# Chunked attention and a gated feed-forward layer in one kernel: blocks cut along the batches, v of block 1 loaded in two parts around a quarter of w_out, and AV of block 1 in other PSUM banks

## The chip, the cores and the metric

The kernel runs on one core of a Trainium2 chip. The metric is device time in microseconds (us) of one execution. Executions that follow each other differ by one to three us here (the kernel before took 308.97 to 311.54 us in one group of runs), so kernels are compared by several executions on the same chip. All executions told of here were classed as fast; none is compared with a slow one. The profile is one such execution; its span runs from the core's first to its last instruction and is about 2 us shorter than the time (308.6 of 310.3 us for the kernel before).

Names: TensorE (PE) multiplies matrices, and its weight loads (PEld) are listed apart; VectorE is DVE, ScalarE is ACT, GpSimd is POOL, SyncE is SP, which issues most of the loads here. In PSUM the kernel uses eight banks; it calls four of them A and four F.

## The reference

Softmax attention inside chunks of 64 tokens, then a feed-forward layer with a Swish gate:

```python
batch, n_heads, seq, head_dim = (8, 8, 576, 64)      # 9 chunks of 64 in a batch
scores = 1 / sqrt(64) * (q_c @ k_c.T)                # for each chunk by itself
attn = softmax(scores); x = (attn @ v_c)             # x: 4608 tokens x 512
h = x @ w_in                                         # w_in: 512 x 2048
g = h * sigmoid(beta * h)
out = g @ w_out                                      # w_out: 2048 x 512, out: 4608 x 512
```

All inputs and the output are float32 in HBM. The kernel casts to bfloat16 on the chip.

## The kernel before

The 72 chunks are worked in nine blocks of 8 chunks (512 tokens). A block needs: loads of q, k, v; casts on POOL; transposes of q and k (on TensorE for blocks 0 to 2; later by DMA, after which POOL or DVE copies the result into order); scores; exp; AV (attn @ v); normalisation on DVE; a transpose ("turn") of x; then 16 groups of four matmuls on w_in (`mm1`) and 16 groups of four on w_out (`mm2`). From block 2 on, the attention of a block is woven into the matmul groups of earlier blocks. Blocks 0 and 1 come while weights and inputs still arrive.

Every operation is recorded with a time in a schedule (`at(time, ...)`); sorted by it, the operations form one queue for each engine, and each engine runs its queue in order. Tiles that one engine writes and another reads become semaphore waits.

Before the change, blocks follow the running number of the chunk. A batch has 9 chunks, so most blocks straddle two batches, and a pair of chunks that does so is loaded as two DMAs of 64 partitions each ("half-height") instead of one of 128:

```python
def chunk_runs(blk):
    g, end, runs = 8 * blk, 8 * blk + 8, []
    while g < end:
        b, c = divmod(g, CPB)                 # CPB = 9 chunks in a batch
        n = min(end - g, CPB - c)
        runs.append((b, c, n, g - 8 * blk))
        g += n
    return runs

def chunk_pairs(blk):
    out = []
    for b, c, n, at in chunk_runs(blk):
        end = at + n
        while at < end:
            m = 2 if at % 2 == 0 and at + 2 <= end else 1
            out.append((b, c, m, at))
            at, c = at + m, c + m
    return out
```

AV of a block comes in two parts (u = 0, 1: heads 0 to 3 and 4 to 7), each of 32 small matmuls that write all four banks of A. Normalisation reads these banks and writes x:

```python
def attend(blk, u, ps=A, psname="A"):
    sa = blk % NVA
    for cc in range(4):
        ... # hb, w, g: 8 matmuls of 64x64 by 64x65
                P.op("pe", f, reads=[K("E", 2 * u + hb, v=blk), K("v_bf", sa, cc, v=blk),
                                     K("ones", sa)],
                     writes=[K(psname, 2 * g + cc // 2, v=("o", blk, u))])

def normalize(blk, u, ps=A, psname="A"):
    ... # DVE: reciprocal of the row sums, then one tensor_tensor into x_sb
```

The schedule of block 1 and of the weights that matters here:

```python
for j in range(4):
    at(-97, load_w_in, j)
    at((-43, 1.5, 5.5, 9.5)[j], cast_w_in, j, ("pool",) * 4)
    at((-42, 1.7, 5.7, 9.7)[j], load_w_out, j)
    at((16.1, 20, 24, 25)[j], cast_w_out, j, ("pool",) * 4)
at(-43.5, load_qk, 1, 0)
at(-43.5, load_qk, 1, 1)
at(-43.5, load_v, 1)
...
for blk, t in ((1, 10), (2, 28)):
    for i in range(4):
        at(25 if blk == 2 else t + 0.1 * i, cast_qk, blk, i // 2, i % 2, "pool")
        at(t + 0.9 * i if blk == 2 else 10.5 + 0.8 * i, transpose_pe, blk, i // 2, i % 2, A, "A", ("act", "dve")[i % 2])
        at(26 if blk == 2 else t + 4, cast_v, blk, "pool", i)
for hp in range(4):
    at(14.9 + 0.6 * (hp // 2), scores, 1, hp)
for bank in range(4):
    at((15.1, 15.2, 15.7, 15.8)[bank], exp, 1, bank)
at(17.1, attend, 1, 0)
at(17.2, normalize, 1, 0)
at(18.1, attend, 1, 1)
at(18.2, turn_pe, 1, 0, F, "F", 0, "act")
at(18.3, normalize, 1, 1)
at(19.1, turn_pe, 1, 1, F, "F", 1, "act")
```

The recorder notes every operation that reads a tile, so that whoever overwrites the tile later waits for all its readers. Each such reader counts up its engine's semaphore:

```python
for key, v in writes:
    add(self.writer.get(key), op["queue"] == "pool")
    for r in self.readers.get(key, ()):
        add(r, False)
for key, v in reads:
    self.readers.setdefault(key, []).append(op)
```

The softmax here doesn't subtract the row's maximum and nothing guards it: scores larger than these inputs give would overflow.

## Time and profile before

| | before |
|---|---|
| time, median of three (lowest to highest) | 310.36 us (310.19 to 310.51) |
| profiled span | 308.6 us |
| TensorE busy from 31.8 to 51.8 us | 12.58 of 20 us |
| TensorE busy from 100 to 120 us | 19.74 of 20 us |

From the page of the kernel before: the clock granted to TensorE in tenths over 40 slices of 7.7 us, and the chain of work that ended last, as shares of the span by engine and by line.

```profile
PEclk9999985999999999999999999999999999999999
...
PE 80%; SPq 9%; DMA 6%; issue 1%; POOL 1%; DVE 1%; ACT 0%
PE F L456 40%; PE F L441 36%; SPq L257 6%; DMA wstage<-in_moe_w_out_dram 4%; DMA vstage<-in_v_dram 2%; SPq L265 2%; PE A L389 2%; PE A L367 2%; SPq L274 1%; POOL w_out_bf L306 1%; PE A L341 1%; DVE x_sb L405 0%; PE A L423 0%; DVE g L449 0%; ACT tt L446 0%
```

The chain is TensorE's (L456 and L441 are the two feed-forward matmuls), except for a stretch of loads at the start. And the clock drops in one place, between 39 and 54 us (by the trace's records to half, from 43.7 to 53.9 us). The table of stretches shows the same place from another side; its columns are named in its first line.

```profile
core 0: us, PE busy (x) PEld busy (x) DVE busy (x) ACT busy (x) POOL busy (x), PEclk, DMA share, GB/s
31.80:51.80 20.00, 12.58 (x201) 7.31 (x201) 10.02 (x13) 10.00 (x15) 11.94 (x19) 0.80 1.00 291
100.00:120.00 20.00, 19.74 (x181) 9.18 (x183) 10.38 (x16) 9.39 (x15) 13.11 (x11) 1.00 0.70 183
```

Late in the kernel nothing is to be won: TensorE is full. Early, over 7 us are idle. TensorE's timeline of that place follows; the columns are start, duration, engine, line, operation, tiles, shape, count, and in brackets the idle time before it and what ended it. L367 are scores, L389 AV, L423 turns.

```profile
40.32 0.44 PE L367 MATMUL A<-qkO 64*64 64x64 bf16 x32
41.75 0.19 PE L389 MATMUL A<-v_bf,E 64*64 64x65 bf16 x1 [0.98 <-ACT E L374]
42.63 0.32 PE L389 MATMUL A<-v_bf,E 64*64 64x65 bf16 x16 [0.69 <-ACT E L374]
43.12 0.32 PE L389 MATMUL A<-v_bf,E 64*64 64x65 bf16 x15 [0.17 <-ACT E L374]
45.48 0.66 PE L389 MATMUL A<-v_bf,E 64*64 64x65 bf16 x32 [2.04 <-DVE x_sb L405]
46.07 1.03 PE L423 MATMUL F<-identity,x_sb 128*128 128x128 bf16 x8
48.41 1.03 PE L423 MATMUL F<-identity,x_sb 128*128 128x128 bf16 x8 [1.31 <-DVE x_sb L405]
49.23 1.06 PE L441 MATMUL F<-xT,w_in_bf 128*128 128x512 bf16 x2
50.55 1.04 PE L441 MATMUL F<-xT,w_in_bf 128*128 128x512 bf16 x2 [0.26 <-ACT xT L312]
```

AV part 0 writes the A banks while exp still reads scores from them, so it follows the exps bank by bank. AV part 1 waits 2.04 us until normalisation of part 0 has emptied A. The turns wait for their own normalisations. Nothing else is in TensorE's queue there.

This stretch also begins late, for the last keys of block 1 come late. POOL's timeline:

```profile
35.60 1.04 POOL L314 CAST qkcast<-qkstage 128x1024 bf16<-128x1024 f32 x1 [1.35 <-DMA qkstage<-in_k_dram]
```

### The profile page before, as it was taken

To read this page: it belongs to the slowest core of one execution; us is meant where nothing else is said; L and a number is where in the kernel's file an instruction comes from. 1 tells how busy PE (TensorE), PEld (TensorE's weight loads), DVE (VectorE), ACT (ScalarE), POOL (GpSimd) and SP (SyncE) were. 2 spreads that over 40 slices of the span, in tenths; PEclk is the share of its full clock that TensorE was granted. 3 is DMA by queue.
4 is the path that set the end of the run, shared out by engine and by line. 5 is a ranking of instruction groups with operands and counts; after the bars stand their busy time and mean duration, and the time that the engine had idled before them with its cause. 6 is when DMAs were issued, how large, how long until landed. Compare 5 with 4: busy or idle time off the path is not lost.

```text
span 308.6 us, 5739 instructions
## 1 busy us (share of the span) xinstructions
PE 281.7 (91%) x2415; PEld 134.9 (44%) x2448; DVE 137.2 (44%) x194; ACT 150.6 (49%) x230; POOL 117.0 (38%) x130
## 2 busy tenths in 40 slices
PE   1679747999899999999999999999999999999995
PEld 1444423454444444444444444444444444444442
DVE  1347742353573643364346436533553364434300
ACT  2537643456356444745464446455544645455411
POOL 1348548742490674077229220951570000000000
PEclk9999985999999999999999999999999999999999
DMA  7999999989999389929964997499531022000121
GB/s 198 273 385 328 180 346 368 250 257 234 240 291 219 88 211 270 203 68 286 244 155 102 294 202 189 78 340 230 127 79 36 34 70 69 36 34 34 38 100 68
DMA packets 106153, 55.96 MB, mean 181 GB/s; under 512 B 78992, under 2 KB 97424, under 8 KB 106128
## 3 DMA queue, kind: packets, MB, share of 16 engines
q1 hardware_dynamic: 98880, 46.15, 61.7%
q10 hardware_dynamic: 7248, 9.45, 8.9%
q8 instruction: 19, 0.31, 0.4%
q14 instruction: 6, 0.05, 0.1%
HBM read 36.71 MB, written 9.44 MB: 150 GB/s over the span
## 4 chain that ended last, share of the span: by engine, by line
PE 80%; SPq 9%; DMA 6%; issue 1%; POOL 1%; DVE 1%; ACT 0%
PE F L456 40%; PE F L441 36%; SPq L257 6%; DMA wstage<-in_moe_w_out_dram 4%; DMA vstage<-in_v_dram 2%; SPq L265 2%; PE A L389 2%; PE A L367 2%; SPq L274 1%; POOL w_out_bf L306 1%; PE A L341 1%; DVE x_sb L405 0%; PE A L423 0%; DVE g L449 0%; ACT tt L446 0%
## 5 line engine op out<-in xcount | busy, mean ns | idle before, releaser
L449 DVE SCALAR_TENSOR_TENSOR g<-tt,F 128x512 bf16<-128x512 bf16 x144 | 98.9, 687 | 128.9 <-ACT tt L446 128.7
L446 ACT ACTIVATE tt<-F,beta_half 128x512 bf16<-128x512 f32 x144 | 98.9, 687 | 116.9 <-PE F L441 113.0
L441 PE MATMUL F<-xT,w_in_bf 128*128 128x512 bf16 x576 | 148.3, 383 | 0.9 <-DVE g L449 0.6
L456 PE MATMUL F<-w_out_bf,g 128*128 128x512 bf16 x543 | 140.3, 381 | 2.6 <-issue 1.1
L456 PEld LDWEIGHTS F<-w_out_bf,g 128*128 128x128 bf16 x576 | 56.1, 99 | 67.4 <-issue 1.4
L441 PEld LDWEIGHTS F<-xT,w_in_bf 128*128 128x128 bf16 x576 | 54.3, 98 | 64.4 <-issue 1.7
L314 POOL COPY qkO<-qkT 128x1024 bf16<-128x1024 bf16 x22 | 42.7, 1981 | 59.6 <-DMA qkT<-qkcast 28.9
L314 POOL CAST qkcast<-qkstage 128x1024 bf16<-128x1024 f32 x32 | 34.7, 1092 | 27.0 <-DMA qkstage<-in_q_dram 13.2
L461 ACT ACTIVATE ostage<-F 128x512 f32<-128x512 f32 x36 | 21.5, 597 | 18.6 <-PE F L456 18.4
L314 POOL CAST v_bf<-vstage 128x512 bf16<-128x512 f32 x36 | 21.1, 611 | 14.9 <-DMA vstage<-in_v_dram 14.9
L374 ACT ACTIVATE E<-A 128x512 bf16<-128x512 f32 x36 | 20.6, 591 | 1.8 <-PE A L367 1.4
L405 DVE TENSOR_TENSOR x_sb<-A,rec 128x1024 bf16<-128x1024 f32 x17 | 20.8, 1224 | 0.6
L389 PE MATMUL A<-v_bf,E 64*64 64x65 bf16 x544 | 8.6, 200 | 4.1 <-ACT E L374 2.1
L341 PE MATMUL F<-identity,qkcast 128*128 128x128 bf16 x32 | 4.1, 311 | 8.3 <-DVE qkcast L314 6.4
L294 POOL CAST w_in_bf<-wstage 128x512 bf16<-128x512 f32 x16 | 9.1, 613 | 5.4 <-DMA wstage<-in_moe_w_in_dram 5.4
L306 POOL CAST w_out_bf<-wstage 128x512 bf16<-128x512 f32 x16 | 9.1, 613 | 5.1 <-DMA wstage<-in_moe_w_out_dram 5.1
L389 PEld LDWEIGHTS A<-v_bf,E 64*64 64x64 bf16 x544 | 6.3, 111 | 10.7 <-issue 6.6
L367 PEld LDWEIGHTS A<-qkO 64*64 64x64 bf16 x576 | 6.8, 112 | 8.2 <-issue 5.7
L367 PE MATMUL A<-qkO 64*64 64x64 bf16 x576 | 8.7, 200 | 1.2 <-ACT qkO L312 1.2
L402 DVE RECIPROCAL rec<-A 128x16 f32<-128x16 f32 x17 | 4.3, 254 | 7.4 <-PE F L441 4.0
L312 ACT ACTIVATE xT<-F 128x1024 bf16<-128x1024 bf16 x3 | 3.1, 1023 | 8.2 <-PE F L423 8.2
L341 PEld LDWEIGHTS F<-identity,qkcast 128*128 128x128 bf16 x32 | 3.1, 141 | 9.0 <-DVE qkcast L314 6.8
(31 smaller groups left out, 46.7 us busy)
## 6 DMA issues: line engine op xcount, KB each, us to landing
out_dram<-ostage ACTq DMA_DIRECT2D x36, 256.0 KB, 2.1
qkstage<-in_q_dram SPq DMA_DIRECT2D x32, 256.0 KB, 4.4
qkstage<-in_k_dram SPq DMA_DIRECT2D x32, 256.0 KB, 5.2
vstage<-in_v_dram SPq DMA_DIRECT2D x32, 256.0 KB, 6.5
wstage<-in_moe_w_in_dram SPq DMA_DIRECT2D x4, 1024.0 KB, 10.6
wstage<-in_moe_w_out_dram SPq DMA_DIRECT2D x4, 1024.0 KB, 10.6
qkstage<-in_q_dram SPq DMA_DIRECT2D x8, 128.0 KB, 4.6
qkstage<-in_k_dram SPq DMA_DIRECT2D x8, 128.0 KB, 5.1
```

Of the source, the lines that this page charges most:

```text
L257: return e.dma_start(qkstage[r:r + 64 * m, s, which, :, at // 2, :], a)
L306: P.op(eng, lambda e, d=dst, a=src: e.tensor_copy(d, a), reads=[K("wstage", s, v=4 + j)], writes=[K("w_out", 4 * j + i)])
L314: P.op(eng, lambda e: e.tensor_copy(dst, src), reads, writes)
L367: return e.matmul(A[64 * g:64 * g + 64, 2 * u + hb, col:col + 64], kT[r, 2 * cc + g, :], qT[r, 2 * cc + g, :])
L374: P.op("act", lambda e: e.activation(E[:, bank, :], A[:, bank, :], AF.Exp, scale=0.125), reads=[K("A", bank, v=("s", blk))], writes=[K("E" ...
L389: return e.matmul(ps[64 * half:64 * half + 64, bank, col:col + 65], E[r, 2 * u + hb, 256 * w + 64 * cc:256 * w + 64 * cc + 64], v_bf[r, sa ...
L405: P.op("dve", lambda e: e.tensor_tensor(x_sb[:, u, :, :, :].rearrange("p g c (h d) -> p (g c h) d", h=2).rearrange("p (b t) d -> p b t d", ...
L441: P.op("pe", lambda e, c=c: e.matmul(F[:, bank, :], w_in_bf[:, c, 128 * t:128 * t + 128], x_of(sx, c), start=(c == 0), stop=(c == NC - 1)) ...
L446: P.op("act", lambda e: e.activation(tt[:, T % 3, :], F[:, bank, :], AF.Tanh, scale=beta_half[:, t:t + 1]), reads=[K("F", bank, v=("h", T) ...
L449: P.op("dve", lambda e: e.scalar_tensor_tensor(g2[:, sg, t, :], tt[:, T % 3, :], 1.0, F[:, bank, :], ALU.add, ALU.mult), reads=[K("F", ban ...
L456: P.op("pe", lambda e, t=t: e.matmul(F[:, bank, :], g2[:, sg, t, 128 * s:128 * s + 128], w_out_bf[:, t, :], start=(t == 0), stop=(t == NT ...
L461: P.op("act", lambda e: e.activation(ostage[:, N % NOS, :], F[:, bank, :], AF.Copy, scale=0.5), reads=[K("F", bank, v=("o", N))], writes=[ ...
```

## The change

The intent, as read from the diff: (1) make blocks equal to batches (their first 8 chunks), with one block, number 5, for the eight last chunks, so that blocks 0 to 4 and 6 to 8 are loaded without half-height DMAs; (2) load v of block 1 in two parts, with the first quarter of w_out between them; (3) write AV part 0 of block 1 to the F banks, which are idle there (in the trace before nothing uses them from 41.84 us, the end of a gate product, to the turn at 46.07), so that it need not wait for all exps nor hold up part 1; (4) fill waits of that attention with two early groups on w_out. The output rows follow the new blocks.

```diff
+        REST = 5
         def chunk_pairs(blk):
-            ... (walks over chunk_runs)
+            if blk == REST:
+                return [(b, CPB - 1, 1, b) for b in range(B)]
+            return [(blk - (blk > REST), c, 2, c) for c in range(0, 8, 2)]
-        def load_v(blk):
+        def load_v(blk, us=(0, 1)):          # the heads of parts us alone; cast_v likewise
         ... (keys of vstage and v_bf now name the part u; output rows by batch)
-            at((-42, 1.7, 5.7, 9.7)[j], load_w_out, j)
-            at((16.1, 20, 24, 25)[j], cast_w_out, j, ("pool",) * 4)
+            at((-42.8, 1.7, 5.7, 9.7)[j], load_w_out, j)
+            at((15, 20, 24, 25)[j], cast_w_out, j, ("pool",) * 4)
-        at(-43.5, load_v, 1)
+        at(-42.9, load_v, 1, (0,))
+        at(-42.7, load_v, 1, (1,))
-                at(t + 0.9 * i if blk == 2 else 10.5 + 0.8 * i, transpose_pe, ...)
-                at(26 if blk == 2 else t + 4, cast_v, blk, "pool", i)
+                at(t + 0.6 + 0.9 * i if blk == 2 else 10.5 + 0.8 * i, transpose_pe, ...)
+                if blk == 2:
+                    at(26, cast_v, 2, "pool", i)
+                else:
+                    at(t + 4, cast_v, 1, "pool", i, (0,))
+                    at(t + 6.5, cast_v, 1, "pool", i, (1,))
-            at(14.9 + 0.6 * (hp // 2), scores, 1, hp)
+            at(15.4, scores, 1, hp)
-            at((15.1, 15.2, 15.7, 15.8)[bank], exp, 1, bank)
-        at(17.1, attend, 1, 0)
-        at(17.2, normalize, 1, 0)
+            at(15.5 + 0.1 * bank, exp, 1, bank)
+        at(17.1, attend, 1, 0, F, "F")
+        at(17.2, normalize, 1, 0, F, "F")
-            at(24.5 + (0, 0, 3.5, 3.6)[n] if n < 4 else 24.5 + n, mm2, 0, s, part, 2 + s % 2)
+            at((18.5, 19.5, 24.5, 24.6)[n] if n < 4 else 24.5 + n, mm2, 0, s, part, 2 + s % 2)
```

More of the change, by code (lines that the diff above doesn't have):

```diff
@@ L200, in bass_chunk_attention__then__act_swish_beta_kernel @@
         F = es.enter_context(nc.psum_tensor("F", [128, 4, 512], F32))
-        def chunk_runs(blk):
-            g, end, runs = 8 * blk, 8 * blk + 8, []
-            while g < end:
-                b, c = divmod(g, CPB)
-                n = min(end - g, CPB - c)
-                runs.append((b, c, n, g - 8 * blk))
-                g += n
-            return runs
-        def chunk_pairs(blk):
-            out = []
-            for b, c, n, at in chunk_runs(blk):
-                end = at + n
-                while at < end:
-                    m = 2 if at % 2 == 0 and at + 2 <= end else 1
-                    out.append((b, c, m, at))
-                    at, c = at + m, c + m
-            return out
+        REST = 5
+        def chunk_pairs(blk):
+            if blk == REST:
+                return [(b, CPB - 1, 1, b) for b in range(B)]
+            return [(blk - (blk > REST), c, 2, c) for c in range(0, 8, 2)]
         def make_constants():
@@ L258, in load_qk @@
                 P.dma(queue, f, writes=[K("qkstage", s, which, at + i, v=blk) for i in range(m)])
-        def load_v(blk):
-            s = blk % NVS
+        def load_v(blk, us=(0, 1)):
+            s, h = blk % NVS, slice(4 * us[0], 4 * us[-1] + 4)
             for b, c, m, at in chunk_pairs(blk):
@@ L264, in f @@
                     r = 64 * (at % 2)
-                    return e.dma_start(vstage[r:r + 64 * m, s, at // 2, :, :],
-                                       v[b][:, 64 * c:64 * (c + m), :].rearrange("h t d -> t h d"))
-                P.dma("sp", f, writes=[K("vstage", s, at + i, v=blk) for i in range(m)])
+                    return e.dma_start(vstage[r:r + 64 * m, s, at // 2, h, :],
+                                       v[b][h, 64 * c:64 * (c + m), :].rearrange("h t d -> t h d"))
+                P.dma("sp", f, writes=[K("vstage", s, u, at + i, v=blk)
+                                       for u in us for i in range(m)])
         def load_w_in(j):
@@ L350, in transpose_pe, with cast_v @@
                       [K("qkO", hp, which, half, v=blk) for hp in range(4)])
-        def cast_v(blk, eng, cc):
-            s, sa = blk % NVS, blk % NVA
-            copy_cast(eng, v_bf[:, sa, cc, :, 0:64], vstage[:, s, cc, :, :],
-                      [K("vstage", s, 2 * cc + g, v=blk) for g in range(2)],
-                      [K("v_bf", sa, cc, v=blk)])
+        def cast_v(blk, eng, cc, us=(0, 1)):
+            s, sa, h = blk % NVS, blk % NVA, slice(4 * us[0], 4 * us[-1] + 4)
+            copy_cast(eng, v_bf[:, sa, cc, h, 0:64], vstage[:, s, cc, h, :],
+                      [K("vstage", s, u, 2 * cc + g, v=blk) for u in us for g in range(2)],
+                      [K("v_bf", sa, u, cc, v=blk) for u in us])
         def scores(blk, hp):
@@ L392, in f @@
                                     v_bf[r, sa, cc, 4 * u + 2 * w + hb, 0:65])
-                            P.op("pe", f, reads=[K("E", 2 * u + hb, v=blk), K("v_bf", sa, cc, v=blk),
+                            P.op("pe", f, reads=[K("E", 2 * u + hb, v=blk), K("v_bf", sa, u, cc, v=blk),
                                                  K("ones", sa)],
@@ L463, in mm2 @@
                      reads=[K("F", bank, v=("o", N))], writes=[K("o", N % NOS, v=N)])
-                n0 = 512 * blk + 128 * s
-                P.dma("act", lambda e: e.dma_start(out[n0:n0 + 128, :], ostage[:, N % NOS, :]),
+                rows = out.rearrange("(b t) d -> b t d", b=B)
+                if blk == REST:
+                    rows = rows[2 * s:2 * s + 2, 512:S, :]
+                else:
+                    rows = rows[blk - (blk > REST), 128 * s:128 * s + 128, :]
+                P.dma("act", lambda e: e.dma_start(rows, ostage[:, N % NOS, :]),
                       reads=[K("o", N % NOS, v=N)])
@@ L516, in bass_chunk_attention__then__act_swish_beta_kernel @@
                 at(25 if blk == 2 else t + 0.1 * i, cast_qk, blk, i // 2, i % 2, "pool")
-                at(t + 0.9 * i if blk == 2 else 10.5 + 0.8 * i, transpose_pe, blk, i // 2, i % 2, A, "A", ("act", "dve")[i % 2])
-                at(26 if blk == 2 else t + 4, cast_v, blk, "pool", i)
+                at(t + 0.6 + 0.9 * i if blk == 2 else 10.5 + 0.8 * i, transpose_pe, blk, i // 2, i % 2, A, "A", ("act", "dve")[i % 2])
+                if blk == 2:
+                    at(26, cast_v, 2, "pool", i)
+                else:
+                    at(t + 4, cast_v, 1, "pool", i, (0,))
+                    at(t + 6.5, cast_v, 1, "pool", i, (1,))
         for hp in range(4):
-            at(14.9 + 0.6 * (hp // 2), scores, 1, hp)
+            at(15.4, scores, 1, hp)
         for bank in range(4):
-            at((15.1, 15.2, 15.7, 15.8)[bank], exp, 1, bank)
-        at(17.1, attend, 1, 0)
-        at(17.2, normalize, 1, 0)
+            at(15.5 + 0.1 * bank, exp, 1, bank)
+        at(17.1, attend, 1, 0, F, "F")
+        at(17.2, normalize, 1, 0, F, "F")
         at(18.1, attend, 1, 1)
```

## The prediction

> **What bounds the kernel now.** TensorE. The chain of waits gives it 80% of the 308.6 us span. By the table of stretches it is over 97% busy from 100 us on (0.86 us per four-matmul group). The loss is early: TensorE is busy 12.58 of the 20 us from 31.8 to 51.8. By the timeline it waits 1.75 us at 34.9 (last key cast on GpSimd, released by its load), then from 40.7 to 49.2 it only takes pieces of block 1's attention. AV part 0 writes the four A banks, so it waits for all four exps (43.1); AV part 1 waits 2.0 us for part 0's normalisation to empty A; the turns wait for normalisations. The records grant half a TensorE clock from 43.7 to 53.9 us. [...] the seven w_out matmuls at 51.8 take 2.73 us.
>
> Loads are the second limit. By the landings, block 1 needs q and k until 35.5 and v until 39.6 us, with six of its 15 loads half-height (64 partitions), and v in 256-byte packets at about 217 GB/s against 350 for q and k and 385 for weights. Half-height v loads run at 150, then a hole at 35 us. w_out lands at 44.1, 46.8, 49.4, 52.2.
>
> **What the change does.** Arithmetic and bytes stay. Block 1 needs 8 full-height q/k loads instead of 10, and v in two halves around the first w_out quarter. Estimates from these rates and durations:
> - last key landed at 33, cast by 34.4 instead of 36.6: about 1.5 us;
> - v half 0 landed by 36, first w_out quarter 38–39.5, v half 1 40–41.5, the last quarter about 49 instead of 52;
> - AV part 0 into F starts when exps 0 and 1 are done; AV part 1 into A no longer waits for normalisation, but for exps 2 and 3 and for the cast of v half 1 behind four w_out casts (2.3 us): about 42.4 us instead of 46.1;
> - two w_out groups (0.86 us each) fill the waits for normalisation and turns; two more follow.
>
> TensorE then reaches the first transposes of block 2 at about 54 instead of 57.8 us with four more groups (3.5 us) done. That is 7 us, all critical, if the clock stays whole; a quiet window still halving it (chance 0.3) loses about 2.5 us again.
>
> Later: the half-height loads gather in block 5 (24 of 128 KB). That block's data had about 8 us in hand before its scores; the extra issues (0.6 us each) cost about 4. Block 3's transposed q and k landed at 81.1 and will be about 4 us earlier, while TensorE comes 7 us earlier.
>
> **Predicted: 303.8 us, range 301.3 to 306.8.** Faster by over 2% 0.55, within 2% 0.43, slower 0.02.
>
> **What would show it.** Right: TensorE busy 31.8–51.8 rises to 15–17 us; the 2.0 us wait of AV on x_sb is gone; no half clock, or a shorter one; last w_out quarter by 50 us. Wrong: AV part 1 long waiting for v_bf; half clock still about 10 us; new waits at block 3's order copies (near 80 us) or at block 5's scores (near 142 us).
>
> **What would make it wrong.** The first w_out quarter delaying v half 1; the clock; DVE blocked on block 3's transpose, which holds up its g work in order.

The passage cut from it, where the cut is marked, gave a rule for the clock. No term of its sum is cut: the 7 us, and the 2.5 us at a chance of 0.3, stand. What the trace of the kernel before shows of the clock: from 40.27 to 43.68 us TensorE is busy 1.32 of 3.41 us, and its clock is half for the 10.24 us after that; the seven w_out matmuls of 2.73 us begin in it, and the eight w_in matmuls that follow them, at the full clock again from 54.38 us on, took 1.89. The chance of 0.3 and the cost of about 2.5 us are estimates, and the prediction does not say from which numbers. The rates of the loads are those of the landings in the same trace: in block 0, v loads of 256 KB land 1.2 us apart (217 GB/s) and most q and k loads 0.75 us apart (350), and the later quarters of w_out, 1 MB each, land 2.7 us apart (385). While the half-height v loads of block 1 run, from 32.5 to 34.5 us, the table of stretches gives 136 to 170 GB/s, and 31 from 35.0 to 35.5 us.

## The result, and the profile after

Ratios below are the mean time of one kernel's fast runs over that of the other's fast runs of the same rounds, so they are not quite the ratio of the medians that stand beside them.

| | before | after |
|---|---|---|
| time, median (lowest to highest) | 310.38 us (310.19 to 310.51, 4 runs) | 305.75 us (305.31 to 307.16, 4 runs) |
| ratio to before, 95% interval | | 0.9859 (0.9827 to 0.9892) |
| profiled span | 308.6 us | 303.5 us |
| TensorE busy from 31.8 to 51.8 us | 12.58 us | 17.86 us |
| half clock near 43 us | 10.2 us | 3.4 us |

The changed kernel is 4.6 us faster, inside the predicted range and 2 us short of its middle. The gain is 1.4%, so it lies in the class "within 2%", to which the prediction gave 0.43, and not in "over 2%", to which it gave 0.55. The same lines of the page after:

```profile
PEclk9999989999999999999999999999999999999999
...
PE 88%; DVE 3%; ACT 3%; DMA 2%; issue 1%; SPq 1%; ACTq 0%
PE F L432 41%; PE F L447 40%; PE A L358 3%; PE A L380 2%; DVE x_sb L396 2%; DMA qkstage<-in_k_dram 2%; SPq L247 1%; PE A L332 1%; PE F L414 1%; ACT E L365 1%; ACT tt L437 1%; DVE g L440 1%; PE F L380 1%; DVE qkO L305 0%; ACTq L460 0%
```

The chain no longer runs over loads of v and w_out; of its loads only k is left with a share. The stretches after:

```profile
31.80:51.80 20.00, 17.86 (x223) 10.46 (x221) 10.39 (x15) 11.44 (x17) 13.85 (x26) 0.91 1.03 318
100.00:120.00 20.00, 19.84 (x181) 9.30 (x184) 8.85 (x13) 9.07 (x15) 14.10 (x12) 1.00 0.69 185
```

TensorE's timeline after (L358 scores, L380 AV, L414 turns, L447 w_out, L432 w_in):

```profile
37.83 1.51 PE L358 MATMUL A<-qkO 64*64 64x64 bf16 x64
39.80 0.22 PE L380 MATMUL F<-v_bf,E 64*64 64x65 bf16 x4 [0.46 <-POOL w_out_bf L297]
40.24 0.52 PE L380 MATMUL F<-v_bf,E 64*64 64x65 bf16 x28 [0.22 <-ACT E L365]
41.45 1.29 PE L380 MATMUL A<-v_bf,E 64*64 64x65 bf16 x32 [0.69 <-POOL v_bf L305]
42.99 0.91 PE L414 MATMUL F<-identity,x_sb 128*128 128x128 bf16 x8 [0.25 <-DVE x_sb L396]
44.12 1.48 PE L447 MATMUL F<-w_out_bf,g 128*128 128x512 bf16 x3 [0.22 <-issue]
45.40 1.06 PE L414 MATMUL F<-identity,x_sb 128*128 128x128 bf16 x8
46.26 1.19 PE L447 MATMUL F<-w_out_bf,g 128*128 128x512 bf16 x4
47.28 1.03 PE L432 MATMUL F<-xT,w_in_bf 128*128 128x512 bf16 x4
```

The wait of 2.04 us before AV part 1 is gone; part 1 now waits 0.69 us for the cast of the second half of v, and is then held to the pace of its four casts. (The "POOL w_out_bf" before AV part 0 is an attribution to read with care: this AV does not read w_out at all, and the casts of its half of v had ended by 36.3 us, so that wait is for an exp.) The loads came as estimated: by the trace's landing times the last key at 33.2 us (35.5 before), the first half of v at 35.9, the first quarter of w_out at 38.7, the second half of v at 40.8, and the last quarter of w_out at 49.8 (52.2 before).

From there on, TensorE keeps what it won but for one new wait before the scores of block 2:

```profile
60.66 0.61 PE L332 MATMUL A<-identity,qkcast 128*128 128x128 bf16 x8
61.10 1.03 PE L447 MATMUL F<-w_out_bf,g 128*128 128x512 bf16 x4
61.97 1.03 PE L432 MATMUL F<-xT,w_in_bf 128*128 128x512 bf16 x4
63.81 0.45 PE L358 MATMUL A<-qkO 64*64 64x64 bf16 x32 [0.81 <-DVE qkO L305]
```

DVE's timeline after shows why. The last transposes (L332) are done at 61.3 us, but DVE, which runs its queue in order, first has to do a gate product (L440) that itself waits for ACT, and only then copies the keys (L305):

```profile
61.93 0.69 DVE L440 SCALAR_TENSOR_TENSOR g<-tt,F 128x512 bf16<-128x512 bf16 x1 [1.84 <-ACT tt L437]
62.54 1.22 DVE L305 COPY qkO<-A 128x1024 bf16<-128x1024 bf16 x1
```

The order is the diff's doing: it moved the transposes of block 2 by 0.6 in the schedule, which put the last one, and the copy after it, behind one more group on w_in.

The comparison is simplest with three marks from the traces, which split the early part of the kernel: the start of block 1's scores, the start of block 3's scores, and the end. From block 3's scores to the end every kernel here needs 218 to 219 us, apart from the last experiment (219.4).

| trace | scores of block 1 start | from there to scores of block 3 | half clock in that stretch |
|---|---|---|---|
| before | 38.98 | 51.04 | 10.2 |
| after | 37.83 | 46.85 | 3.4 |

So 1.15 us come from arriving earlier at block 1's scores and 4.19 us from the stretch after it.

### The profile page after: what moved, and what is told of

The parts are those of the page before. It is cut to its first block, busy times and chain, and to the rows that moved or that the text cites. A ratio compares the mean times of both kernels' runs of the same rounds, so it can differ in the third digit from the quotient of the medians.

```text
span 303.5 us, 5750 instructions
## 1 busy us (share of the span) xinstructions
PE 280.7 (92%) x2415; PEld 135.4 (45%) x2448; DVE 136.8 (45%) x194; ACT 151.0 (50%) x230; POOL 117.6 (39%) x134
## 4 chain that ended last, share of the span: by engine, by line
PE 88%; DVE 3%; ACT 3%; DMA 2%; issue 1%; SPq 1%; ACTq 0%
PE F L432 41%; PE F L447 40%; PE A L358 3%; PE A L380 2%; DVE x_sb L396 2%; DMA qkstage<-in_k_dram 2%; SPq L247 1%; PE A L332 1%; PE F L414 1%; ACT E L365 1%; ACT tt L437 1%; DVE g L440 1%; PE F L380 1%; DVE qkO L305 0%; ACTq L460 0%
## 5 line engine op out<-in xcount | busy, mean ns | idle before, releaser
L440 DVE SCALAR_TENSOR_TENSOR g<-tt,F 128x512 bf16<-128x512 bf16 x144 | 98.7, 686 | 127.6 <-ACT tt L437 127.4
L432 PE MATMUL F<-xT,w_in_bf 128*128 128x512 bf16 x576 | 146.5, 380 | 0.7 <-DVE g L440 0.6
L447 PE MATMUL F<-w_out_bf,g 128*128 128x512 bf16 x543 | 140.4, 381 | 2.7 <-issue 1.3
L447 PEld LDWEIGHTS F<-w_out_bf,g 128*128 128x128 bf16 x576 | 55.8, 98 | 65.4 <-issue 0.8
L432 PEld LDWEIGHTS F<-xT,w_in_bf 128*128 128x128 bf16 x576 | 54.2, 98 | 64.7 <-DVE g L440 2.0
L305 POOL COPY qkO<-qkT 128x1024 bf16<-128x1024 bf16 x22 | 42.7, 1984 | 59.6 <-DMA qkT<-qkcast 20.3
L305 POOL CAST qkcast<-qkstage 128x1024 bf16<-128x1024 f32 x32 | 33.0, 1046 | 24.8 <-DMA qkstage<-in_k_dram 9.9
L305 POOL CAST v_bf<-vstage 128x512 bf16<-128x512 f32 (+1 forms) x40 | 23.4, 616 | 14.0 <-DMA vstage<-in_v_dram 13.8
L396 DVE TENSOR_TENSOR x_sb<-A,rec 128x1024 bf16<-128x1024 f32 x16 | 19.6, 1224 | 0.6
L332 PE MATMUL F<-identity,qkcast 128*128 128x128 bf16 x32 | 4.1, 311 | 8.6 <-DVE qkcast L305 6.9
L358 PEld LDWEIGHTS A<-qkO 64*64 64x64 bf16 x576 | 7.5, 112 | 8.7 <-issue 5.3
L358 PE MATMUL A<-qkO 64*64 64x64 bf16 x576 | 9.3, 199 | 2.0 <-ACT qkO L303 1.2
L380 PEld LDWEIGHTS A<-v_bf,E 64*64 64x64 bf16 x512 | 5.9, 109 | 7.8 <-issue 5.5
L380 PE MATMUL A<-v_bf,E 64*64 64x65 bf16 x512 | 8.2, 198 | 1.2 <-POOL v_bf L305 0.7
L332 PEld LDWEIGHTS F<-identity,qkcast 128*128 128x128 bf16 x32 | 3.1, 141 | 9.4 <-DVE qkcast L305 7.1
## 6 DMA issues: line engine op xcount, KB each, us to landing
wstage<-in_moe_w_in_dram SPq DMA_DIRECT2D x4, 1024.0 KB, 10.2
```

Source lines behind the costliest of these rows:

```text
L305: P.op(eng, lambda e: e.tensor_copy(dst, src), reads, writes)
L332: P.op("pe", lambda e, n=n, i=i: e.transpose(dst[:, i, n, :], qkcast[:, which, 2 * half + n, i, :, :].rearrange("p h d -> p (h d)"), ident ...
L358: return e.matmul(A[64 * g:64 * g + 64, 2 * u + hb, col:col + 64], kT[r, 2 * cc + g, :], qT[r, 2 * cc + g, :])
L380: return e.matmul(ps[64 * half:64 * half + 64, bank, col:col + 65], E[r, 2 * u + hb, 256 * w + 64 * cc:256 * w + 64 * cc + 64], v_bf[r, sa ...
L396: P.op("dve", lambda e: e.tensor_tensor(x_sb[:, u, :, :, :].rearrange("p g c (h d) -> p (g c h) d", h=2).rearrange("p (b t) d -> p b t d", ...
L432: P.op("pe", lambda e, c=c: e.matmul(F[:, bank, :], w_in_bf[:, c, 128 * t:128 * t + 128], x_of(sx, c), start=(c == 0), stop=(c == NC - 1)) ...
```

## The experiments

Two theories stood at the start. Theory M: the gain is mainly the reordered attention of block 1 (F banks, early w_out groups, order), and the loads matter less. Rival D: it is mainly the earlier and better loads of the aligned blocks. Then there was the question why the gain was smaller than the 7 us that the prediction counted. Candidates were the half clock, the new wait before block 2's scores, and a third found in the trace: the counts of TensorE's semaphore.

Each run was timed in five rounds. The runs of one group ran on one chip: 1 to 4, then 5 to 8, then 9 to 12, with medians of before of 309.34, 310.26 and 310.30 us (11 runs each). All gave correct results.

### 1. Only the aligned blocks (e1_align)

The kernel before, with the change's `chunk_pairs` and output rows and nothing else.

> The kernel before with only the new cut into blocks (blocks equal to batches, one block of last chunks); order of block 1, its v in one part and AV in the A banks stay. Theory M (the gain comes mainly from the reordered attention of block 1): the last key is cast about 2 us earlier (34.4 instead of 36.6 us), so about 1.5 to 2 us shorter, 308.5 us, and the wait of AV part 1 on normalisation stays near 2.0 us and the half clock near 10 us. Rival D (the gain is the earlier loads): 4 us or more shorter, 306.5 us or less.

Measured: 308.81 us, ratio 0.9963 (0.9938 to 0.9987), so about 1.1 us shorter. In the trace, scores of block 1 start at 37.48 us, 1.5 us before the kernel before; from there to block 3's scores it takes 51.50 us, no less than before. The half clock lasts 10.2 us and AV part 1 waits 2.0 us for normalisation, as in the kernel before. The loads bring the start of the stretch forward and nothing more. Rival D falls.

### 2. Everything but the aligned blocks (e2_reorder)

The changed kernel with `chunk_runs`, the old `chunk_pairs` and the old output rows.

> The changed kernel with the old cut into blocks: v of block 1 in two parts, AV part 0 into F, the early w_out groups and the new order all stay. Theory M: 2.5 to 3.5 us shorter than before, about 307.3 us, the half clock as short as in the changed kernel. Rival D: under 1 us shorter, since the last key comes as late as before and everything waits behind it.

Measured: 306.51 us, ratio 0.9895 (0.9872 to 0.9918), about 3.3 us shorter. Scores of block 1 start at 39.15 us, as late as before, and the stretch from there takes 46.85 us, exactly that of the changed kernel. The two parts add up: 1.1 and 3.3 us make the 4.4 us that the ratio 0.9859 of the whole stands for. (The later measurement of the whole, run 5, gives 3.5 us; the sum agrees with both only within the intervals.) Theory M holds.

### 3. Transposes of block 2 back by one group (e3_transpose_back)

```diff
-                at(t + 0.6 + 0.9 * i if blk == 2 else ...
+                at(t + 0.9 * i if blk == 2 else ...
```

> The changed kernel with the transposes of block 2 moved back by one group, so that DVE copies the last keys before its next gate product and not after. If the 0.81 us wait of block 2's scores on that copy is a loss that reaches the end: 0.7 to 0.9 us shorter than the changed kernel, about 304.9 us, and the wait gone. If it is covered by something later: no difference.

Measured: 305.62 us, ratio 0.9865 (0.9835 to 0.9896): no difference from the changed kernel. The profile tells that the wait before the scores is gone and another has come, at the first of these transposes:

```profile
55.22 0.62 PE L332 MATMUL A<-identity,qkcast 128*128 128x128 bf16 x8 [0.77 <-POOL qkcast L305]
```

Its cast stands in POOL's queue behind the casts of the last w_out quarter, which landed at 51.8 us in this execution and at 49.8 us in that of the changed kernel. So the expectation failed, and for a reason of its own: all four transposes were moved ahead, where only the last needed it. Run 6 is the mended trial.

### 4. Fewer semaphore counts (e4_last_signal)

Of the matmuls that read one tile, only the last remains a reader in the recorder's books, so only it counts up the semaphore. This is safe only if matmuls end in order. That they do was the assumption; what the runs show of it is that the results of runs 4, 11 and 12, which count in this way, were correct. In the attention of block 1 in both traces the counts of TensorE's semaphore come 34 ns apart over rows of small matmuls (from 38.1 to 40.2 us in the kernel after, over the scores).

```diff
         for key, v in reads:
-            self.readers.setdefault(key, []).append(op)
+            held = self.readers.setdefault(key, [])
+            if op["queue"] == "pe":
+                held[:] = [r for r in held if r["queue"] != "pe"]
+            held.append(op)
```

> The changed kernel, but of the matmuls of a group that read one tile only the last one counts up TensorE's semaphore. In both traces these counts come 34 ns apart, so 32 small matmuls hold the next engine for 1.08 us after a start that the matmuls themselves need 0.45 us for. Theory S (the counts, not the matmuls, are what exp and normalisation wait for): the first exp of block 1 starts about 0.45 us earlier after the scores, the reciprocal about 1 us earlier after AV part 0, the 1.5 us wait before block 2's turn falls to about 0.8 us; in all 0.8 to 1.5 us shorter than the changed kernel, about 304.6 us. Rival: the small matmuls themselves need that time, and nothing moves (305.7 us).

Measured: 304.11 us, ratio 0.9817 (0.9791 to 0.9842), four runs between 303.96 and 304.37 us. By the ratios that is 1.3 us shorter than the changed kernel's first measurement (2.2 us against the later one, run 5); the trace agrees, with 45.33 instead of 46.85 us from scores to scores. ACT's timeline of the changed kernel and, below it, TensorE's and ACT's of this run:

```profile
39.10 2.18 ACT L365 ACTIVATE E<-A 128x512 bf16<-128x512 f32 x4 [0.48 <-PE A L358]
```

```profile
38.01 0.76 PE L361 MATMUL A<-qkO 64*64 64x64 bf16 x64
```

```profile
38.70 2.05 ACT L368 ACTIVATE E<-A 128x512 bf16<-128x512 f32 x4
```

After the first score matmul the first exp comes 0.69 us later instead of 1.27. The 64 score matmuls themselves take 0.76 us instead of 1.51: the counts had slowed not only those who wait for them but the matmuls too. They did so only in the long row: by the records of the changed kernel the first 33 of the 64 start within 0.27 us and the others 34 ns apart, and rows of 32 score matmuls (those of block 2) take 0.45 us with the counts and 0.44 without. In the kernel before, the scores of block 1 stood in two such rows (0.45 and 0.44 us), so this loss came with the change's new order. From the first AV matmul to the reciprocal it is 1.07 us instead of 1.61 (1 us less was expected), and the wait before block 2's turns fell from 1.47 to 0.82 us. Theory S holds. (The first w_in matmul of block 0 also came 1.3 us earlier, at 20.1 us. That was given back: TensorE now waits 0.8 us for the casts of block 1's keys, which did not come sooner.)

### 5. The changed kernel again (e5_changed_again)

> The changed kernel once more, as the control of this group of runs on the same chip: ratio to before between 0.983 and 0.989, half a clock granted once for 3.4 us near 43 us.

Measured: 306.96 us (305.10 to 308.22, 6 runs), ratio 0.9888 (0.9854 to 0.9922), so a gain of 3.5 us here where the first measurement gave 4.4. The profiled execution had the half clock for 6.8 us, not 3.4, and took 47.50 us from scores to scores instead of 46.85. Each run lists its mean granted clock. With spans of 304 us, a mean of 0.994 is 3.4 us at half clock, 0.988 is 6.8 us. Of the ten timed executions of this kernel, one had none, four had about 3.4 us and five about 6.8 us. They took 305.87 us; 305.10 to 305.87 us; and 306.85 to 308.22 us. So the expectation of one window was wrong, and much of the spread between runs goes with this count. Not all of it: the one execution without half clock was no shorter than those with one window. The kernel before varies as well: of its 33 executions in the three groups, 17 had about 6.8 us (mean 309.6 us) and 16 about 10.2 us (mean 310.6 us), and the profile shown above is one of the latter kind. The start goes with it: where the trace first grants the full clock at 22.4 to 22.7 us, scores of block 1 start at 37.5 to 37.9 us (after, runs 1 and 8); at 24.6 to 24.9 us, they start at 38.7 to 39.0 us (runs 5 to 7).

### 6. Only the last transpose of block 2 moved ahead (e6_last_transpose)

```diff
-                at(t + 0.6 + 0.9 * i if blk == 2 else ...
+                at(t + (0, 0.9, 1.8, 2.3)[i] + 0.6 if blk == 2 else ...
```

> The changed kernel, where only the last of the four transpose groups of block 2 goes ahead of one group of w_in matmuls, so that DVE copies the last keys before the next gate product. The cast that this transpose reads ended 3.6 us before it in the trace. Theory (the 0.81 us wait of the scores of block 2 reaches the end): that wait is gone, and 0.7 to 0.9 us shorter than the changed kernel of this group. Rival (it is made up for later, or another wait takes its place as when all four were moved): within 0.3 us of it.

Measured: 305.33 us, ratio 0.9842 (0.9813 to 0.9870), 1.4 us below the control by the ratios; the intervals overlap, so the size is better read from the trace: 45.97 us from scores to scores, 0.88 less than the changed kernel, with the same 3.4 us of half clock. The wait is gone. DVE copies right after the transposes, and TensorE goes on without a gap:

```profile
61.65 1.23 DVE L305 COPY qkO<-A 128x1024 bf16<-128x1024 bf16 x1 [0.35 <-PE A L332]
```

```profile
64.14 0.45 PE L358 MATMUL A<-qkO 64*64 64x64 bf16 x32
```

So the new wait was a loss of the change itself, and it did reach the end.

### 7. Useless matmuls to hold the clock (e7_filler)

15 matmuls of 252 columns on weights that are already there, four before AV part 0, five after it, and two before each further quarter of AV part 1. In the trace five of them in a row took 0.71 us and four 0.60, so 0.11 us for one more. They write columns of PSUM banks that no other engine touches at that time.

```diff
+        at(17.0, filler, 4, F, 2, True)
         at(17.1, attend, 1, 0, F, "F")
         at(17.2, normalize, 1, 0, F, "F")
-        at(18.1, attend, 1, 1)
+        at(18.05, filler, 3)
+        at(18.1, attend, 1, 1, A, "A", 2)     # two more before each quarter
```

> The changed kernel with 15 useless matmuls of 252 columns (about 0.1 us each, results overwritten) put in the waits around AV of block 1, to keep TensorE active there. Theory C (the half clock from 43 to 46.6 us is caused by the quiet 3.4 us before it, and costs about 1.5 us): no half clock there, first matmul on w_out and second turn sooner, 1.0 to 1.5 us shorter than the changed kernel of this group. Rival (the work there is bound by normalisation and casts, the clock costs little): the half clock may go, but under 0.4 us is won.

Measured: 305.34 us (304.53 to 305.98, 6 runs), ratio 0.9844 (0.9820 to 0.9867), 1.4 us below the control by the ratios. The mean granted clock was 1.0 in all six runs. From scores to scores: 45.78 us, so 1.07 less than the trace with 3.4 us of half clock and 1.72 less than the trace with 6.8 us. In the traces the clock changes in steps of 3.41 us (half clock for 3.41 us in the changed kernel, 6.83 in run 5, 10.24 in the kernel before), so the windows to look at are those between two such steps. Run 5 and this run stand at nearly the same phase: their windows begin 0.34 and 0.28 us before the scores of block 1. The lines below, from the table of stretches, are the window just before the clock fell in the changed kernel (1.94 us busy), the same in run 5 (2.56 us busy), and the two windows of this run that cover the same work (3.21 and 3.36 us busy), after which the clock stayed full.

```profile
39.75:43.16 3.41, 1.94 (x67) 1.30 (x68) 1.67 (x3) 1.52 (x3) 2.68 (x7) 1.00 0.99 345
```

```profile
38.39:41.80 3.41, 2.56 (x98) 1.91 (x96) 1.90 (x4) 2.75 (x6) 3.30 (x8) 1.00 1.16 291
```

```profile
38.50:41.92 3.42, 3.21 (x105) 2.48 (x104) 1.84 (x4) 2.76 (x6) 3.42 (x8) 1.00 1.13 285
41.92:45.33 3.41, 3.36 (x53) 1.79 (x52) 2.51 (x4) 1.02 (x2) 2.04 (x5) 1.00 1.06 402
```

So filling these windows held the clock in all six executions, as theory C says. Busy time alone does not decide it, however. In the kernel before, the following window was less busy than either of those that cost the clock, and full clock came after it:

```profile
33.45:36.86 3.41, 1.66 (x19) 0.96 (x17) 2.42 (x3) 2.25 (x4) 2.06 (x3) 1.00 0.81 133
```

All its 19 matmuls have weights of 128 by 128; of the 98 in run 5's window 96 have weights of 64 by 64. What decides it, no run here shows.

By the traces the half clock costs 1.1 us when it lasts one window and 1.7 us when it lasts two. These sizes come from single traces, and the useless matmuls take some TensorE time themselves; the one execution of the changed kernel without half clock (305.87 us, no trace kept) does not show the gain. So it is shown that filling the windows held the clock here, and what the half clock costs is known only roughly.

### 8. No early w_out groups (e8_no_fill)

```diff
-            at((18.5, 19.5, 24.5, 24.6)[n] if n < 4 else 24.5 + n, mm2, ...)
+            at((24.5, 24.5, 28.0, 28.1)[n] if n < 4 else 24.5 + n, mm2, ...)
```

> The changed kernel without the early w_out groups between the turns of block 1: both come after the first w_in group, as before. Theory M (they fill waits for normalisation): 1 to 2.5 us longer than the changed kernel of this group, with new idle of TensorE before the second turn. Rival: no change, since the turns come sooner instead.

Measured: 308.04 us, ratio 0.9926 (0.9894 to 0.9958), about 1.2 us longer than the control by the ratios, at the low end of what was expected, with intervals that overlap. In the trace it is 47.42 us from scores to scores, 0.57 more than the changed kernel at the same half clock, and TensorE waits again before the turns:

```profile
42.82 1.02 PE L414 MATMUL F<-identity,x_sb 128*128 128x128 bf16 x8 [0.72 <-DVE x_sb L396]
44.24 1.03 PE L414 MATMUL F<-identity,x_sb 128*128 128x128 bf16 x8 [0.40 <-DVE x_sb L396]
```

The mean granted clock of its other five executions was 0.987 to 0.989, two windows at half clock, where the control had two windows in four of its six. The groups fill waits; that they help to hold the clock is not shown by five against four of six.

### 9. AV part 0 in the A banks (e9_av_in_a)

```diff
-        at(17.1, attend, 1, 0, F, "F")
-        at(17.2, normalize, 1, 0, F, "F")
+        at(17.1, attend, 1, 0)
+        at(17.2, normalize, 1, 0)
```

> The changed kernel with AV part 0 of block 1 written to the A banks again. Theory M (F frees the chain: AV part 0 need not wait for the last two exps, AV part 1 need not wait until normalisation has emptied A): AV part 0 starts or ends 0.5 to 1 us later, AV part 1 waits about 2 us for normalisation again, second turn about 2 us later; in all 1.5 to 3 us longer than the changed kernel, ratio to before about 0.994, half clock longer. Rival: the cast of v half 1 holds AV part 1 anyway, so under 0.7 us.

Measured: 307.62 us, ratio 0.9908 (0.9884 to 0.9933). The group had no control; against the two ratios of the changed kernel (0.9859 and 0.9888) it is 0.6 to 1.5 us longer, and the intervals overlap with the later one. From scores to scores 47.71 us, 0.86 more at the same half clock. The wait is back as expected:

```profile
43.85 0.65 PE L380 MATMUL A<-v_bf,E 64*64 64x65 bf16 x32 [2.13 <-DVE x_sb L396]
```

Its cost is below the 1.5 to 3 us that were expected and, by the trace, a little above the rival's 0.7. That fits with the wait of 0.69 us in the changed kernel, where the cast of v holds part 1 for a while in its place.

### 10. v of block 1 whole, before w_out (e10_v_whole)

```diff
-        at(-42.9, load_v, 1, (0,))
-        at(-42.7, load_v, 1, (1,))
+        at(-43.5, load_v, 1)
-                    at(t + 4, cast_v, 1, "pool", i, (0,))
-                    at(t + 6.5, cast_v, 1, "pool", i, (1,))
+                    at(t + 4, cast_v, 1, "pool", i)
```

> The changed kernel with v of block 1 loaded and cast in one part before the first w_out quarter. AV part 1 no longer waits for GpSimd behind four w_out casts (about 0.7 us less wait), but the w_out quarter lands near 41 instead of 38.5 us and is cast by about 43.3, so the first w_out group comes then. Theory M: those two nearly balance, within 0.8 us of the changed kernel (ratio 0.984 to 0.990). Rival (the split carries the gain): 1.5 us or more longer.

Measured: 305.87 us, ratio 0.9871 (0.9841 to 0.9901); 46.86 us from scores to scores, against 46.85. Splitting v made no difference that these runs can show. AV part 1 came sooner (its only wait is 0.26 us, for an exp) and the w_out quarter landed at 41.9 instead of 38.7 us. Counted from the scores, the second turn came 0.9 us sooner than in the changed kernel, but the w_out group after it stood at the half clock (in the kernel before, seven w_out matmuls took 2.73 us at the half clock, and the eight w_in matmuls after them 1.89), and the first w_in group of block 1 came after 9.3 us instead of 9.5.

### 11. Last signals and the last transpose together (e11_signal_and_transpose)

> The changed kernel with the counting of only the last matmul of a group (as in the run of the last signal) and the last transpose group of block 2 moved ahead (as in that run). If the two are independent: 1.9 to 2.4 us shorter than the changed kernel, 303.3 us, ratio to before about 0.979.

Measured: 303.52 us (303.13 to 304.75, 6 runs), ratio 0.9793 (0.9767 to 0.9819). From scores to scores 44.82 us, 2.03 less than the changed kernel. The two single gains were 1.52 and 0.88 us in the traces, together 2.40, so most of both remains. This is the version to keep: it beats both kernels, by about 6.4 us and by about 2 to 3 us.

### 12. Both, and the useless matmuls (e12_all_three)

> The same with the 15 useless matmuls around AV of block 1 as well. If the clock's loss is still there without them (half clock 3.4 us or more in the run before this one): another 1 us shorter, about 302.3 us, ratio to before about 0.975, clock 1.0 in all runs. If the shorter chain leaves no room for them: no better than without.

Measured: 303.83 us, ratio 0.9791 (0.9765 to 0.9817), the mean granted clock 0.998 to 1.0. No better than run 11. By block 2's scores the trace is 0.54 us ahead of run 11's (24.06 us from the scores of block 1, against 24.60). Then TensorE met the limit that the prediction had feared for the change itself, the copies that put block 3's transposed keys and queries in order:

```profile
82.99 0.45 PE L361 MATMUL A<-qkO 64*64 64x64 bf16 x32 [0.73 <-POOL qkO L308]
...
85.75 0.45 PE L361 MATMUL A<-qkO 64*64 64x64 bf16 x32 [0.48 <-POOL qkO L308]
```

The trace of run 11 has no such wait. TensorE came to these scores only 0.26 us earlier than there (82.26 us without the wait, against 82.52), but block 3's transposes landed at 79.98 us instead of 78.45. Why they landed later is open; with one trace of each, so is whether the wait would come in every execution. In this trace it used up what the clock had gained.

The traces side by side (us; half clock is that of the profiled execution alone):

| run | scores of block 1 start | to scores of block 3 | half clock | ratio to before |
|---|---|---|---|---|
| before | 38.98 | 51.04 | 10.2 | 1 |
| after | 37.83 | 46.85 | 3.4 | 0.9859 |
| e1_align | 37.48 | 51.50 | 10.2 | 0.9963 |
| e2_reorder | 39.15 | 46.85 | 3.4 | 0.9895 |
| e3_transpose_back | 38.69 | 47.06 | 3.4 | 0.9865 |
| e4_last_signal | 38.01 | 45.33 | 3.4 | 0.9817 |
| e5_changed_again | 38.73 | 47.50 | 6.8 | 0.9888 |
| e6_last_transpose | 39.03 | 45.97 | 3.4 | 0.9842 |
| e7_filler | 38.78 | 45.78 | 0 | 0.9844 |
| e8_no_fill | 37.66 | 47.42 | 3.4 | 0.9926 |
| e9_av_in_a | 37.90 | 47.71 | 3.4 | 0.9908 |
| e10_v_whole | 38.41 | 46.86 | 3.4 | 0.9871 |
| e11_signal_and_transpose | 37.70 | 44.82 | 3.4 | 0.9793 |
| e12_all_three | 37.91 | 45.08 | 0 | 0.9791 |

## Why the prediction was right, and where it was off

**The bound was right.** TensorE sets the time, only the part before 60 us could shrink, and nothing changed after it: from block 3's scores to the end, 218.6 us before and 218.8 us after.

**The loads were right.** The prediction had the last key landed at 33 us and cast by 34.4; measured 33.2 and 34.4. It had the halves of v by 36 and at 40 to 41.5 us, the first and last w_out quarters at 38 to 39.5 and about 49; measured 35.9, 40.8, 38.7 and 49.8. The 1.5 us for it is 1.15 in the trace, and 1.1 by run 1.

**The mechanism was right.** The wait of 2.0 us on normalisation went, AV part 1 ended near 42.4 us as foreseen (42.7), the early groups filled waits. Runs 2, 8 and 9 show that this carries most of the gain: 3.3 us by run 2. By the traces run 9 puts F at about 0.9 us and run 8 the early groups at 0.6 us, each with the same 3.4 us of half clock; run 10 leaves nothing for the split of v. These three were undone one at a time, so they need not add up; what the rest of the 4.2 us is made of (a shorter half clock, fewer interruptions in the w_in groups before the scores) was not taken apart.

**The size was too large by two terms.** The prediction counted 7 us "all critical, if the clock stays whole". Its first mark, the first transposes of block 2 "at about 54" us, was at 55.0, so that 6.2 us were won there (2.8 us and four groups of 0.86); then the new copy wait took 0.8.
- *The half clock.* The prediction gave it a chance of 0.3 and a cost of 2.5 us. It came in nine of ten executions and cost 1.1 us for one window and 1.7 us for two (run 7 against the traces of the changed kernel). The chance was the error, and as far as run 7 tells the cost was put too high. The prediction does not say what the chance rests on. The groups and turns that it lists as filling waits come from 42.99 us on, and the window that half clock followed in the trace, 39.75 to 43.16 us, lay before them.
- *The copy before block 2's scores.* It was not in the prediction at all. The shift of the transposes by 0.6 stood in the diff, and the listing of DVE's queue showed a gate product more before the copy. Its cost is 0.8 to 0.9 us by the trace (runs 3 and 6).

Taking both away from the stretch of the changed kernel leaves 46.85 - 0.88 - 1.07 = 44.90 us, 6.1 less than before; with the 1.15 us of the earlier start that is 7.3 us. So by this addition the sum of 7 us was about right for what it described, and the two terms are what was missing. That is worked out and not shown: the two removals were each run, but not together without a third edit, and in run 12, which has all three, part of the gain was lost again.

**Where luck helped.** The median lies in the range, but the same kernel measured again (run 5) had a median of 306.96 us, just outside 301.3 to 306.8. Four of those six executions had two windows at half clock, against one of the four of the first measurement.

**What it feared and did not come.** Block 3's transposes landed at 78.8 us, 2.3 us earlier than before where about 4 had been expected, and its scores at 84.68 us did not wait. They do in run 12 but not in run 11, though TensorE is over 2 us earlier in both. Block 5's half-height loads cost about what was estimated: its ordered keys were ready 8.5 us before its scores in the kernel before, and 5.0 us before them after. Its 24 loads of 128 KB were issued one every 0.6 to 0.7 us but for one gap, and q, k and v took 20 us to land from the first issue, against 17 us for the straddling block before.

## What to carry to other kernels

When a chain of small steps on several engines stands in front of a busy engine, look at what else can be put into that engine's queue there, and whether a free PSUM bank lets two steps overlap: that, not the faster loads, carried this change (3.3 us by run 2, against 1.1 us for the loads by run 1). Every shift in a schedule also reorders the queues of the other engines, so list each queue before and after and ask of each pair that changed places what the second now waits behind. Try counting up a semaphore only at the last of a row of small matmuls: here the counts came 34 ns apart, and with fewer of them a row of 64 score matmuls took 0.76 us instead of 1.51 and the kernel 1.3 us less (run 4), while rows of 32 took 0.44 us instead of 0.45. And look at the windows of 3.41 us between the steps of the clock: here half clock followed one with TensorE busy for 1.94 us (the changed kernel) and one with 2.56 us, 96 of its 98 matmuls on 64x64 weights (run 5), and not those filled to 3.21 and 3.36 us (run 7), nor one with 1.66 us of matmuls on 128x128 weights (the kernel before).
